# Start of a gated-mix kernel: one piece of K's weights loaded on another queue, the gate vector turned by a padded product, reordered first K pieces with shorter fillers

## Chip, cores and metric

The kernel runs on one core of a Trainium2 chip. The metric is the device time of that core in microseconds (us). Engines: PE is TensorE, PEld its weight loads, DVE is VectorE, ACT is ScalarE, POOL is GpSimd, SP is SyncE; "SPq" and "ACTq" are the queues on which SP and ACT issue DMAs.

## The reference

One input x (2048 x 640, bf16) goes through a linear-attention block A and a mixer with an MLP (block B); a gate mixes the two. Only the first lines of A and the gate matter here:

```python
g = sigmoid((x * gate_w).sum(-1, keepdims=True))
qkv = x @ wqkv                      # 640 -> 3 * 640
q, k, v = ...                       # 32 heads of 20
pq, pk = phi(q), phi(k)             # phi(t) = (t + 1 if t > 0 else exp(t)) + 1e-6
...
return g * a + (1 - g) * b
```

The kernel computes K first: for each of 16 chunks of 128 rows of x, `x_chunk @ wk`, as five products of 128 rows of the contraction (five "pieces" of wk). The gate's logit comes along as a 641st column of wk.

## The kernel before

The start, up to the K products, with cuts marked by `[...]`. Chunk 0 of x is loaded plainly and transposed on PE; chunks 1 to 15 come by seven DMA transposes, all on the SP queue.

```python
load_x(0, 1)                                                  # SP queue
aq.dma_start(g5[:], gate_w.rearrange("(c p) -> c p", p=P))    # aq is the ACT queue
load_wk(sp, 1)
load_wk(aq, 0)
load_wk(aq, 2)
load_wk(sp, 3)
load_wk(aq, 4)
for c0, c1 in ((1, 2), (2, 3), (3, 4), (4, 6), (6, 8), (8, 12), (12, 16)):
    load_xT(c0, c1)                                           # DMA transpose, SP queue
[...]
def k_mm(pt, c, dcs, hfs=(0, 1), last=DC - 1):
    for dc in dcs:
        for hf in hfs:
            n = HD + hf
            nc.tensor.matmul(pt[:, hf, 0:n], lhsT=xT[:, dc, c * P:(c + 1) * P],
                             rhs=wk_sb[:, dc, hf * HD:hf * HD + n], start=(dc == 0), stop=(dc == last))
[...]
def warmup(n, w=TS):        # fillers: products of ones that keep PE busy
    for i in range(n):
        nc.tensor.matmul(warm[:, 1, 0:w], lhsT=one[:, 0:P], rhs=one[:, 0:w], start=True, stop=True)

warmup(6)
warmup(3, P)
kp = pair()
turns = [(pair()[:, 0, :].bitcast(BF16), a, b) for a, b in ((0, 2), (2, DC))]
tg = warm[:, 0, :].bitcast(BF16)
for n, (ptb, a, b) in enumerate(turns):
    for dc in range(a, b):
        nc.tensor.transpose(ptb[:, (dc - a) * P:(dc - a + 1) * P], x_sb[:, 0, dc * P:(dc + 1) * P], ident[:])
    nc.vector.tensor_copy(xT[:, a:b, 0:P], ptb[:, 0:(b - a) * P].rearrange("p (c s) -> p c s", c=b - a))
    if n == 0:
        nc.tensor.transpose(tg[:, 0:DC], g5[:], ident[0:DC, 0:DC])
        nc.vector.tensor_copy(wk_sb[:, :, D], tg[:, 0:DC])
warmup(3, P)
for dc in range(DC):
    k_mm(kp, 0, (dc,))
    if dc < DC - 1:
        warmup(1, 2 * P)
k_evac(kp, 0)
for c in range(1, NCH):
    pt = pair()
    k_mm(pt, c, range(DC))
    k_evac(pt, c)
```

After K come the Q products, then the rest, which the change does not touch.

## Time and profile before

| | before |
|---|---|
| time, median of 3 runs | 265.8 us (265.54 to 266.0) |
| span of the profiled run | 264.0 us |
| first x transpose on PE | 3.66 us |
| first K product / K of chunk 1 / K of chunk 8 | 4.82 / 7.12 / 16.66 us |
| transposed x chunks 8-11 landed | 16.43 us |
| first Q product | 27.56 us |
| full clock granted to PE from | 5.83 us |

Times inside a run count from the start of the span; the landing times are those that the trace records for each DMA. The page of the kernel before begins with the busy time of each engine; its part 4 follows the work that ended last back to its start and gives each engine's share of it:

```profile
span 264.0 us, 4272 instructions
## 1 busy us (share of the span) xinstructions
PE 260.3 (99%) x1744; PEld 161.8 (61%) x1744; DVE 139.5 (53%) x271; ACT 85.1 (32%) x126; POOL 21.9 (8%) x67
...
## 4 chain that ended last, share of the span: by engine, by line
PE 97%; ACT 1%; DVE 0%; issue 0%
```

A chain that is PE to 97% says that what PE starts earlier ends earlier, as long as nothing else comes to be waited for. The timeline of PE in the first 7 us shows what may be saved (start, length, engine, line, operation, tiles, count):

```profile
3.66 0.42 PE L215 MATMUL pp<-ident,x_sb 128*128 128x128 bf16 x2
4.01 0.18 PE L218 MATMUL pp<-ident,g 5*128 5x5 bf16 x1
4.13 0.50 PE L215 MATMUL pp<-ident,x_sb 128*128 128x128 bf16 x3
4.55 0.48 PE L206 MATMUL pp<-const-bfloat16-1.0 128*128 128x128 bf16 x3
4.82 0.74 PE L194 MATMUL pp<-wk_sb,xT 128*128 128x320 bf16 x2
5.36 0.42 PE L206 MATMUL pp<-const-bfloat16-1.0 128*128 128x256 bf16 x1
...
6.74 0.27 PE L206 MATMUL pp<-const-bfloat16-1.0 128*128 128x256 bf16 x1
```

The fillers (L206) stand between the pieces of K (L194). The weight loads of the same stretch show a hole of 0.20 us before the gate vector's, which has 5 rows only:

```profile
3.56 0.25 PEld L215 LDWEIGHTS <-x_sb 128*128 128x128 bf16 x2
4.01 0.10 PEld L218 LDWEIGHTS <-g 5*128 5x128 bf16 x1 [0.20 <-issue]
4.12 0.24 PEld L215 LDWEIGHTS <-x_sb 128*128 128x128 bf16 x3
```

"issue" means that nothing the profile shows was waited for. The timeline of the SP queue shows the first DMA transposes (L121) right behind two pieces of wk (L124):

```profile
0.79 0.39 SPq L118 DMA_DIRECT2D x_sb<-in_A_x_dram  x1
1.25 0.89 SPq L124 DMA_DIRECT2D wk_sb<-in_A_wqkv_dram  x2
2.18 2.73 SPq L121 DMA_TRANSPOSE xT<-in_A_x_dram  x2
```

### The profile page before, as it was taken

To read this page: it belongs to the slowest core of one execution; us is meant where nothing else is said; L and a number is where in the kernel's file an instruction comes from. 1 tells how busy PE (TensorE), PEld (TensorE's weight loads), DVE (VectorE), ACT (ScalarE), POOL (GpSimd) and SP (SyncE) were. 2 spreads that over 40 slices of the span, in tenths; PEclk is the share of its full clock that TensorE was granted. 3 is DMA by queue.
4 is the path that set the end of the run, shared out by engine and by line. 5 is a ranking of instruction groups with operands and counts; after the bars stand their busy time and mean duration, and the time that the engine had idled before them with its cause. 6 is when DMAs were issued, how large, how long until landed. Compare 5 with 4: busy or idle time off the path is not lost.

```text
span 264.0 us, 4272 instructions
## 1 busy us (share of the span) xinstructions
PE 260.3 (99%) x1744; PEld 161.8 (61%) x1744; DVE 139.5 (53%) x271; ACT 85.1 (32%) x126; POOL 21.9 (8%) x67
## 2 busy tenths in 40 slices
PE   8999999999999999999999999999999999999995
PEld 4777555788754654556667555667565576555743
DVE  1688778899948597964503455413356223112132
ACT  1555554321165725612502221412131332142100
POOL 7100120012210040001000001000001000000000
PEclk9999999999999999999999999999999999999999
DMA  7999987016673726700132000051100051100011
GB/s 200 179 208 370 375 252 298 0 29 123 124 101 75 79 51 161 239 0 2 25 75 77 25 0 2 0 99 52 50 0 2 0 101 52 50 0 2 0 50 50
DMA packets 46285, 23.62 MB, mean 89 GB/s; under 512 B 35770, under 2 KB 45626, under 8 KB 46266
## 3 DMA queue, kind: packets, MB, share of 16 engines
q1 hardware_dynamic: 45824, 22.86, 34.1%
q10 hardware_dynamic: 442, 0.49, 0.5%
q8 instruction: 13, 0.21, 0.4%
q14 instruction: 6, 0.05, 0.1%
HBM read 12.21 MB, written 2.62 MB: 56 GB/s over the span
## 4 chain that ended last, share of the span: by engine, by line
PE 97%; ACT 1%; DVE 0%; issue 0%
PE pp L484 21%; PE pp L464 21%; PE pp L194 8%; PE pp L311 8%; PE pp L417 8%; PE pp L448 8%; PE pp L345 8%; PE pp L236 8%; PE pp L206 2%; PE pp L472 1%; PE pp L493 1%; ACT m_sb L385 1%; PE pp L364 1%; PE pp L251 0%; DVE oc L512 0%; PE pp L383 0%
## 5 line engine op out<-in xcount | busy, mean ns | idle before, releaser
L464 PE MATMUL pp<-lnxT,w_sb 128*128 128x512 bf16 x260 | 60.4, 379 | 0.0
L484 PE MATMUL pp<-w_sb,h 128*128 128x256 bf16 (+3 forms) x416 | 58.0, 299 | 0.1
L466 ACT ACTIVATE h<-pp 128x1024 bf16<-128x1024 f32 (+1 forms) x28 | 26.9, 962 | 82.2 <-PE pp L464 82.2
L484 PEld LDWEIGHTS <-h 128*128 128x128 bf16 x416 | 39.3, 98 | 18.0 <-issue 1.3
L464 PEld LDWEIGHTS <-w_sb 128*128 128x128 bf16 x260 | 25.5, 98 | 26.8
L500 DVE SCALAR_TENSOR_TENSOR oc<-pp,omg,x 128x640 bf16<-128x640 f32 x14 | 12.0, 881 | 41.4 <-ACT h2x L475 21.3
L451 DVE SCALAR_TENSOR_TENSOR x<-pp,gate,x 128x640 f32<-128x640 f32 x16 | 13.9, 868 | 29.4 <-PE pp L448 29.4
L420 DVE TENSOR_TENSOR x<-pp,x_sb 128x640 f32<-128x640 f32 x16 | 13.1, 820 | 22.6 <-PE pp L417 22.6
L186 ACT ACTIVATE e<-pp 128x640 bf16<-128x640 f32 (+1 forms) x26 | 21.5, 827 | 9.6 <-PE pp L236 9.6
L448 PE MATMUL pp<-m_sb,pqT 128*128 128x320 bf16 x160 | 24.3, 299 | 0.0
L417 PE MATMUL pp<-w_sb,hsT 128*128 128x320 bf16 x160 | 23.9, 299 | 0.1
L194 PE MATMUL pp<-wk_sb,xT 128*128 128x320 bf16 (+1 forms) x160 | 22.9, 302 | 0.0
L311 PE MATMUL pp<-x_sb,pk 128*128 128x320 bf16 (+1 forms) x160 | 22.3, 300 | 0.0
L236 PE MATMUL pp<-xT,hsT 128*128 128x512 bf16 x100 | 21.7, 379 | 0.0
L311 PEld LDWEIGHTS <-pk 128*128 128x128 bf16 x160 | 18.8, 117 | 3.5
L417 PEld LDWEIGHTS <-hsT 128*128 128x128 bf16 x160 | 15.6, 98 | 8.2 <-issue 0.2
L448 PEld LDWEIGHTS <-pqT 128*128 128x128 bf16 x160 | 15.7, 98 | 7.7
L194 PEld LDWEIGHTS <-xT 128*128 128x128 bf16 x160 | 15.8, 99 | 6.1
L345 PE MATMUL pp<-lnxT,w_sb 128*128 128x512 bf16 x80 | 17.9, 379 | 0.0
L236 PEld LDWEIGHTS <-hsT 128*128 128x128 bf16 x100 | 11.8, 118 | 9.7
L281 POOL TENSOR_SCALAR rstd<-mv 128x4 f32<-128x4 f32 (+1 forms) x11 | 3.4, 314 | 156.5 <-DVE mv L287 156.5
L188 DVE SCALAR_TENSOR_TENSOR pk<-pp,e 128x640 bf16<-128x640 f32 x16 | 13.2, 825 | 1.7
(77 smaller groups left out, 194.9 us busy)
## 6 DMA issues: line engine op xcount, KB each, us to landing
out_dram<-oc SPq DMA_DIRECT2D x14, 160.0 KB, 1.8
w_sb<-in_B_w_dram SPq DMA_DIRECT2D x1, 2080.0 KB, 10.0
w_sb<-in_B_w_dram SPq DMA_DIRECT2D x1, 1296.0 KB, 8.4
x_sb<-in_A_x_dram SPq DMA_DIRECT2D x2, 640.0 KB, 10.4
x_sb<-in_A_x_dram SPq DMA_DIRECT2D x1, 1120.0 KB, 7.9
wo_sb<-in_A_wo_dram SPq DMA_DIRECT2D x6, 160.0 KB, 6.0
w_sb<-in_B_w_dram SPq DMA_DIRECT2D x1, 864.0 KB, 5.7
hsT<-in_A_wqkv_dram SPq DMA_DIRECT2D x1, 800.0 KB, 5.3
```

What stands on the lines that cost most here:

```text
L186: nc.scalar.activation(ev, src, ACT.Exp)
L188: nc.vector.scalar_tensor_tensor(dst, src, 0.0, ev, op0=ALU.max, op1=ALU.add)
L194: nc.tensor.matmul(pt[:, hf, 0:n], lhsT=xT[:, dc, c * P:(c + 1) * P], rhs=wk_sb[:, dc, hf * HD:hf * HD + n], start=(dc == 0), stop=(dc == ...
L236: nc.tensor.matmul(pt[:, t % 2, :], lhsT=wq_sb[:, dc, :].rearrange("p (m j) -> p j m", j=DC)[:, j], rhs=xT[:, dc, t * TS:(t + 1) * TS], st ...
L311: nc.tensor.matmul(pt[:, hf, 0:HD + hf], lhsT=w, rhs=x_sb[:, c, hf * HD:(hf + 1) * HD + hf], start=(c == 0), stop=(c == NCH - 1))
L345: nc.tensor.matmul(pt[:, i, :], lhsT=w, rhs=lnxT[t][:, dc, :], start=(dc == 0), stop=(dc == DC - 1))
L417: nc.tensor.matmul(pt[:, hf, 0:HD], lhsT=hsT[:, fc, 2 + c * P:2 + (c + 1) * P], rhs=w2_sb[:, fc, hf * HD:(hf + 1) * HD], start=(fc == 0), ...
L448: nc.tensor.matmul(pt[:, hf, 0:HD], lhsT=pqT[:, j, c * P:(c + 1) * P], rhs=m_sb[:, j, hf * HD:(hf + 1) * HD], start=(j == 0), stop=(j == D ...
L451: nc.vector.scalar_tensor_tensor(x1, pt[:, :, 0:HD], gate[:, c:c + 1], x1, op0=ALU.mult, op1=ALU.add)
L464: nc.tensor.matmul(pt[:, k, :], lhsT=w3_sb[:, dc, fc * P:(fc + 1) * P], rhs=lnT[:, dc, :], start=(dc == 0), stop=(dc == DC - 1))
L466: nc.scalar.activation(h2[:, 2 * i * TS:(2 * i + n) * TS], pt[:].rearrange("p h e -> p (h e)")[:, 0:n * TS], ACT.Gelu_apprx_tanh)
L484: nc.tensor.matmul(dst, lhsT=st[t]["h2"][:, fc * TS + cc * P:fc * TS + (cc + 1) * P], rhs=w4_sb[:, fc, a:b], start=start and fc == 0, stop ...
```

## The change

The intent is to have PE reach K of chunk 1 earlier: one filler fewer ahead, the gate vector turned without the hole and without a filler waiting for its copy, K's pieces in the order in which they land, shorter fillers between them, and the last piece of wk ahead of the x transposes, so that it lands with the others.

```diff
-    load_wk(aq, 4)
+    load_wk(sp, 4)
[...]
-    def k_mm(pt, c, dcs, hfs=(0, 1), last=DC - 1):
+    def k_mm(pt, c, dcs, first=0, last=DC - 1):
[... start=(dc == first)]
+    k0_order = (1, 0, 3, 2, 4)
[...]
-    warmup(6)
+    nc.vector.memset(g5z[:], 0.0)
+    nc.vector.tensor_copy(g5z[0:DC, :], g5[:])
+    warmup(5)
     warmup(3, P)
     kp = pair()
[... turns keep the whole pair of PSUM banks]
+        if b == DC:
+            nc.tensor.matmul(pt[:, 1, 0:DC], lhsT=g5z[:], rhs=ident[:, 0:DC], start=True, stop=True)
         nc.vector.tensor_copy(xT[:, a:b, 0:P], ptb[:, 0:(b - a) * P].rearrange("p (c s) -> p c s", c=b - a))
-        if n == 0:
-            nc.tensor.transpose(tg[:, 0:DC], g5[:], ident[0:DC, 0:DC])
-            nc.vector.tensor_copy(wk_sb[:, :, D], tg[:, 0:DC])
-    warmup(3, P)
-    for dc in range(DC):
-        k_mm(kp, 0, (dc,))
-        if dc < DC - 1:
-            warmup(1, 2 * P)
+        if b == DC:
+            nc.vector.tensor_copy(wk_sb[:, :, D], pt[:, 1, 0:DC])
+    warmup(4, P)
+    for n, dc in enumerate(k0_order):
+        if n > 1:
+            warmup(1, P)
+        k_mm(kp, 0, (dc,), first=k0_order[0], last=k0_order[-1])
+    warmup(2, P)
```

More of the change, by code (lines that the diff above doesn't have):

```diff
@@ L87 @@
     g5 = const.tile([DC, P], BF16)
+    g5z = const.tile([P, P], BF16)
     mhalf = const.tile([P, CPT], F32)
@@ L188, in phi @@
         nc.vector.scalar_tensor_tensor(dst, src, 0.0, ev, op0=ALU.max, op1=ALU.add)
-    def k_mm(pt, c, dcs, hfs=(0, 1), last=DC - 1):
+    def k_mm(pt, c, dcs, first=0, last=DC - 1):
         for dc in dcs:
-            for hf in hfs:
+            for hf in range(2):
                 n = HD + hf
                 nc.tensor.matmul(pt[:, hf, 0:n], lhsT=xT[:, dc, c * P:(c + 1) * P],
-                                 rhs=wk_sb[:, dc, hf * HD:hf * HD + n], start=(dc == 0), stop=(dc == last))
+                                 rhs=wk_sb[:, dc, hf * HD:hf * HD + n], start=(dc == first), stop=(dc == last))
     def k_evac(pt, c):
@@ L206, in warmup @@
             nc.tensor.matmul(warm[:, 1, 0:w], lhsT=one[:, 0:P], rhs=one[:, 0:w], start=True, stop=True)
-    warmup(6)
+    nc.vector.memset(g5z[:], 0.0)
+    nc.vector.tensor_copy(g5z[0:DC, :], g5[:])
+    warmup(5)
     warmup(3, P)
     kp = pair()
-    turns = [(pair()[:, 0, :].bitcast(BF16), a, b) for a, b in ((0, 2), (2, DC))]
-    tg = warm[:, 0, :].bitcast(BF16)
-    for n, (ptb, a, b) in enumerate(turns):
+    turns = [(pair(), a, b) for a, b in ((0, 2), (2, DC))]
+    for pt, a, b in turns:
+        ptb = pt[:, 0, :].bitcast(BF16)
         for dc in range(a, b):
             nc.tensor.transpose(ptb[:, (dc - a) * P:(dc - a + 1) * P], x_sb[:, 0, dc * P:(dc + 1) * P], ident[:])
+        if b == DC:
+            nc.tensor.matmul(pt[:, 1, 0:DC], lhsT=g5z[:], rhs=ident[:, 0:DC], start=True, stop=True)
         nc.vector.tensor_copy(xT[:, a:b, 0:P], ptb[:, 0:(b - a) * P].rearrange("p (c s) -> p c s", c=b - a))
-        if n == 0:
-            nc.tensor.transpose(tg[:, 0:DC], g5[:], ident[0:DC, 0:DC])
-            nc.vector.tensor_copy(wk_sb[:, :, D], tg[:, 0:DC])
-    warmup(3, P)
-    for dc in range(DC):
-        k_mm(kp, 0, (dc,))
-        if dc < DC - 1:
-            warmup(1, 2 * P)
+        if b == DC:
[6 more added lines that the diff above has]
+    warmup(2, P)
     k_evac(kp, 0)
```

## The prediction

> **What bounds the kernel.** TensorE. The page's chain of work that ended last gives PE 97% of a 264.0 us span; PE is busy 99%. The chain in order of time has PE work without a hole from 7.0 us on. So a gain at the start reaches the end one for one, but only if no later wait eats it. The change touches only the first 7 us (2.7% of the span); a 2% verdict (5.3 us) is out of reach.
>
> **The start now (timeline of PE, DMA landings of the trace).** Warm-up products from 0.83 us; x chunk 0 landed at 3.08; first x transpose 3.66; the 5-row gate turn at 4.01, after a weight-load gap of 0.20 us that the profile calls issue (the gate vector had landed at 2.14, so no data was missing); the next filler began at 4.55, waiting for the DVE copy of the gate column that ended at 4.51. K piece 0 starts at 4.82, piece 4 at 6.85, chunk 1 of K at 7.12. The wk pieces landed: 1 at 4.50, 0 at 4.75, 3 at 5.37, 2 at 5.56, 4 at 6.02. From 4.55 on PE never waits for them: fillers and its own order set the pace. The clock was granted in full only from 5.83.
>
> **Removed.** One cold 512-column filler: 0.43. The row-limited gate turn with its gap and the DVE wait: about 0.14 + 0.13. Fillers in K chunk 0: four of 256 columns become five of 128, about 0.16 net when mostly warm. Added: a DVE memset and copy, hidden, and a 128-row product of 5 columns, under 0.1. Transposes can start at about 3.24. PE then would be ready for K at about 4.27, but piece 1 lands at 4.50, so K starts at about 4.55-4.6. Pieces 1, 0, 3, 2, 4 then run without much waiting; PE is ready for chunk 1 at about 6.75, 0.36 earlier than now.
>
> **What takes it back.** The x transposes are on the SP queue, now behind piece 4 (one SP issue of 0.45 us and 160 KB). The Trainium skill, "DMA: Bandwidth & Descriptors", section "Issuing engines are not separate DMA queues", says the queues share the 16 engines; the trace agrees (DMA 100% busy from 3.5 to 7 us with two queues), so the bytes ahead of the transposes are the same and I estimate a delay of 0 to 0.45 us. Chunk 1 of xT landed at 6.60 (used 7.12). The tightest is chunks 8-11: landed 16.43, used at 16.65, slack 0.22 us only. With PE earlier, chunk 8 becomes DMA-bound: the gain is capped at about 0.17 us minus the delay of the transposes. Net: from 0.2 gained to 0.3 lost.
>
> **Predicted:** 265.6 us, range 265.1 to 266.3; faster by over 2%: 0.01, within 2%: 0.98, slower: 0.01.
>
> **Signs.** Right: transposes near 3.25, no weight-load gap before the gate product, no filler waiting on DVE, K's first piece 4.5-4.6, chunk 1 at 6.75-7.1, and a new PE gap of 0.1-0.6 us before chunk 8 at its landing. Wrong: no gap at chunk 8 and the whole 0.36 us kept; then the transposes' landings moved earlier.
>
> **What could break it.** The Trainium skill, "TensorE: Matmul & The Clock Gate", Part 1, says the clock is released after a busy window of about 3.4 us that runs free of the kernel; here it took 5.0 us from the first product, which agrees. The new idle of 0.25 us before piece 1 might cost a window: K at half speed for another 3.4 us, some 1.5 us lost (a 5% risk). A shift of the window from run to run also moves either kernel by some tenths. Late landing of x shifts everything.

## The result

The changed kernel took 265.88 us in the median of 4 runs, the kernel before 265.70 us in 4 runs. One of the four changed runs, the profiled one, took 704.76 us: PE ran at a little over a third of its pace from beginning to end (most K products start 0.405 us after the one before, where the other runs have 0.136) and the trace holds no clock record at all. It is a slow run and is left out of the times; its three fast companions took 265.69 to 265.98 us (median 265.79). The ratio of the fast runs is 1.0003, 95% interval 0.9984 to 1.0023. A ratio is formed from the mean times of fast runs, so it is not quite the ratio of the medians.

Run again in a later set, beside the kernel before (run e1 below), the change gave 266.35 us against 265.85, ratio 1.0022 (1.0009 to 1.0035). The second is a loss of 0.2% clear of noise. Its profile is used from here on.

```profile
span 264.5 us, 4260 instructions
...
## 4 chain that ended last, share of the span: by engine, by line
PE 91%; SPq 3%; DMA 3%; ACT 1%; issue 1%; DVE 0%
```

The chain is no longer PE alone: 6% of it is now the SP queue and a DMA. (The trace lacks 17 of the 1745 matmul records, so its PE count is not a finding.) The start of PE did what was intended:

```profile
3.23 0.74 PE L219 MATMUL pp<-ident,x_sb 128*128 128x128 bf16 x5
3.77 0.21 PE L221 MATMUL pp<-ident,g5z 128*128 128x5 bf16 x1
3.84 0.59 PE L208 MATMUL pp<-const-bfloat16-1.0 128*128 128x128 bf16 x4
4.21 1.29 PE L195 MATMUL pp<-wk_sb,xT 128*128 128x320 bf16 x4
...
6.88 0.57 PE L195 MATMUL pp<-wk_sb,xT 128*128 128x320 bf16 x3
```

The five transposes follow each other, the padded gate product comes 0.11 us after the last of them starts, the fillers wait for nothing, and K starts 0.61 us earlier (4.21 against 4.82). By chunk 1 the lead is 0.24 us (6.88 against 7.12), since the clock became full later in this run (6.27 us against 5.83): until then K's products stand about 0.27 us apart, afterwards 0.14. No wait for a piece shows in this trace. Ten microseconds on, the timeline shows this:

```profile
15.32 1.25 PE L195 MATMUL pp<-wk_sb,xT 128*128 128x320 bf16 x8
17.18 1.54 PE L195 MATMUL pp<-wk_sb,xT 128*128 128x320 bf16 x10 [0.60 <-DMA xT<-in_A_x_dram]
```

In the same stretch before, PE runs through:

```profile
15.29 3.43 PE L194 MATMUL pp<-wk_sb,xT 128*128 128x320 bf16 x24
```

The product at 17.18 is the first of chunk 8. It starts 0.90 us after the one before it, where 0.136 is the normal distance: 0.76 us lost. The lead of 0.24 has become a lag of 0.52 (17.18 against 16.66); the first Q product lags by 0.53 (28.09 against 27.56), and the span by 0.51. So the account closes: the start gains 0.24, the wait before chunk 8 takes 0.76, and nothing else moves.

The chain in order of time says where that wait comes from (start, length, what):

```profile
...
1.71 0.42 SPq L125
2.14 0.04 issue
2.18 0.43 SPq L125
2.61 0.04 issue
2.66 1.29 SPq L122
...
9.71 7.42 DMA xT<-in_A_x_dram
17.13 0.05 issue
17.18 11.07 PE pp L195 x80
```

It is one row of issues on the SP queue: x, three pieces of wk (L125, the last two are shown), then the transposes (L122, the first is shown), and at last the flight of the transpose of chunks 8-11. The last L125, 0.43 us, is the one that the change put there. The issue of 8-11 began at 9.71 instead of 9.41, 0.30 later, and its flight took 7.42 us instead of 7.03, 0.39 longer; it landed at 17.13 instead of 16.43. In both traces that flight is the longest among the x transposes whose landing is told (view of the tile xT, before and then e1):

```profile
DMA to landing us min/median/max: 3.7/4.6/7.0
```

```profile
DMA to landing us min/median/max: 3.4/4.5/7.4
```

### The profile page after: what moved, and what is told of

Read it like the earlier page. It is cut to its first block, busy times and chain, and to the rows that moved or that the text cites. A ratio compares the mean times of both kernels' runs of the same rounds, so it can differ in the third digit from the quotient of the medians.

```text
span 703.0 us, 4277 instructions
## 1 busy us (share of the span) xinstructions
PE 699.5 (99%) x1745; PEld 281.3 (40%) x1745; DVE 141.4 (20%) x273; ACT 85.7 (12%) x126; POOL 21.6 (3%) x67
## 4 chain that ended last, share of the span: by engine, by line
PE 99%; DVE 0%; issue 0%
PE pp L470 22%; PE pp L490 22%; PE pp L195 9%; PE pp L351 9%; PE pp L317 8%; PE pp L242 8%; PE pp L454 8%; PE pp L423 8%; PE pp L389 1%; PE pp L478 1%; PE pp L499 1%; PE pp L208 1%; PE pp L370 1%; PE pp L257 0%; PE pp L219 0%; PE pp L269 0%
## 5 line engine op out<-in xcount | busy, mean ns | idle before, releaser
L470 PE MATMUL pp<-lnxT,w_sb 128*128 128x512 bf16 x260 | 161.2, 837 | 0.0
L490 PE MATMUL pp<-w_sb,h 128*128 128x256 bf16 (+3 forms) x416 | 155.9, 609 | 0.0
L490 PEld LDWEIGHTS <-h 128*128 128x128 bf16 x416 | 70.7, 173 | 84.4 <-issue 62.7
L470 PEld LDWEIGHTS <-w_sb 128*128 128x128 bf16 x260 | 45.9, 176 | 98.1 <-issue 98.1
L454 PE MATMUL pp<-m_sb,pqT 128*128 128x320 bf16 x160 | 63.4, 610 | 0.0
L423 PE MATMUL pp<-w_sb,hsT 128*128 128x320 bf16 x160 | 62.4, 605 | 0.0
L195 PE MATMUL pp<-wk_sb,xT 128*128 128x320 bf16 (+1 forms) x160 | 60.7, 616 | 0.0
L317 PE MATMUL pp<-x_sb,pk 128*128 128x320 bf16 (+1 forms) x160 | 59.9, 614 | 0.0
L242 PE MATMUL pp<-xT,hsT 128*128 128x512 bf16 x100 | 59.8, 835 | 0.0
L351 PE MATMUL pp<-lnxT,w_sb 128*128 128x512 bf16 x80 | 48.5, 838 | 0.0
L423 PEld LDWEIGHTS <-hsT 128*128 128x128 bf16 x160 | 27.2, 170 | 37.2 <-issue 37.0
L426 DVE TENSOR_TENSOR x<-pp,x_sb 128x640 f32<-128x640 f32 x16 | 13.2, 825 | 109.1 <-PE pp L423 109.1
L242 PEld LDWEIGHTS <-hsT 128*128 128x128 bf16 x100 | 18.7, 187 | 40.4 <-issue 40.4
L351 PEld LDWEIGHTS <-w_sb 128*128 128x128 bf16 x80 | 13.9, 174 | 32.9 <-issue 32.5
```

What stands on the lines that cost most here:

```text
L242: nc.tensor.matmul(pt[:, t % 2, :], lhsT=wq_sb[:, dc, :].rearrange("p (m j) -> p j m", j=DC)[:, j], rhs=xT[:, dc, t * TS:(t + 1) * TS], st ...
L317: nc.tensor.matmul(pt[:, hf, 0:HD + hf], lhsT=w, rhs=x_sb[:, c, hf * HD:(hf + 1) * HD + hf], start=(c == 0), stop=(c == NCH - 1))
L351: nc.tensor.matmul(pt[:, i, :], lhsT=w, rhs=lnxT[t][:, dc, :], start=(dc == 0), stop=(dc == DC - 1))
L423: nc.tensor.matmul(pt[:, hf, 0:HD], lhsT=hsT[:, fc, 2 + c * P:2 + (c + 1) * P], rhs=w2_sb[:, fc, hf * HD:(hf + 1) * HD], start=(fc == 0), ...
L426: nc.vector.tensor_tensor(x1[:].rearrange("p (h e) -> p h e", h=2), pt[:, :, 0:HD], x_sb[:, c, 0:D].rearrange("p (h e) -> p h e", h=2), op ...
L454: nc.tensor.matmul(pt[:, hf, 0:HD], lhsT=pqT[:, j, c * P:(c + 1) * P], rhs=m_sb[:, j, hf * HD:(hf + 1) * HD], start=(j == 0), stop=(j == D ...
```

## The experiments

Three theories stood against each other at first. A: the start gains, and the wait for the transposed x takes it back. B: the start gains nothing, because waits for the pieces took the fillers' place. C: the clock becomes full later. All twelve runs gave correct results. Each profile is one execution, and not always a typical one: it was the fastest of its run's six in e2 and e12 and the slowest in e3, e5 and e6. e1 to e4, e5 to e8 and e9 to e12 ran on one chip each, with the kernel before alongside (medians 265.85, 265.83 and 265.79 us).

| run | full clock | chunk 1 | 8-11 landed | chunk 8 | first Q | median | ratio to before |
|---|---|---|---|---|---|---|---|
| before | 5.83 | 7.12 | 16.43 | 16.66 | 27.56 | | |
| e1 change again | 6.27 | 6.88 | 17.13 | 17.18 | 28.09 | 266.35 | 1.0022 |
| e2 piece 4 on ACT | 4.24 | 6.52 | 16.47 | 16.51 | 27.42 | 266.01 | 1.0005 |
| e3 queue move alone | 5.59 | 7.57 | 17.70 | 17.75 | 28.66 | 266.40 | 1.0018 |
| e4 change, 8-11 split | 5.84 | 6.83 | 15.16 (8-9) | 16.60 | 27.50 | 265.77 | 0.9998 |
| e5 change, short warm-ups | 4.67 | 6.97 | 17.07 | 17.12 | 28.03 | 267.38 | 1.0061 |
| e6 e5 with piece 4 on ACT | 3.97 | 7.09 | 16.95 | 17.00 | 27.91 | 266.96 | 1.0041 |
| e7 before, short warm-ups | 3.84 | 6.66 | 17.40 | 17.45 | 28.36 | 266.92 | 1.0039 |
| e8 five-row gate | 3.44 | 6.66 | 17.22 | 17.27 | 28.18 | 266.35 | one look |
| e9 change, 4-7 merged | 4.56 | 7.72 | 16.43 | 18.48 | 29.38 | 267.59 | 1.0072 |
| e10 e2, 8-11 split | 5.24 | 6.95 | 14.06 (8-9) | 16.50 | 27.39 | 265.69 | 0.9992 |
| e11 e2, 4-7 merged | 6.34 | 6.93 | 15.70 | 17.86 | 28.76 | 267.23 | 1.0050 |
| e12 before, 8-11 split | 3.93 | 6.68 | 14.57 (8-9) | 16.34 | 27.24 | 265.95 | 0.9998 |

In every run in which chunk 8 waits (e1, e2, e3, e5 to e8), it starts 0.04 to 0.05 us after 8-11 landed, whatever chunk 1 did: chunk 1 lies anywhere from 6.52 to 7.57. And the first Q product moves by the later landing minus 0.17 us, the cap that the prediction had worked out. For e1, e2, e3, e5, e6, e7 and e8 that gives +0.53, -0.13, +1.10, +0.47, +0.35, +0.80 and +0.62; measured were +0.53, -0.14, +1.10, +0.47, +0.35, +0.80 and +0.62. This is arithmetic once chunk 8 waits; what the agreement shows is that nothing between chunk 8 and Q waits again.

### e1: the change again

No edit.

> The changed kernel once more, for a profile in the fast state. Theory A (eaten by the x transposes): the first K product starts at 4.5-4.6 us (before 4.82), chunk 1 of K at 6.75-7.1 (before 7.12), but PE stands idle before chunk 8 until its transposed x lands, and chunk 8 starts at 16.5-16.9 (before 16.65), the Q products at 27.6-28.0 (before 27.72). Rival B (nothing gained at the start, waits for the wk pieces took the fillers' place): chunk 1 at 7.0 or later and no idle time before chunk 8. Rival C (clock): the granted clock becomes full later than 5.83 us, so K chunk 0 runs at half pace for longer. All: time within 0.2% of before.

Theory A's picture came, at its far end: the first K product earlier still than expected (4.21, because piece 1 landed at 4.01, not 4.50), chunk 1 at 6.88, chunk 8 at 17.18, above the 16.9 that I had allowed. Rival B falls for the start, since chunk 1 did come earlier. Rival C has a share: the full clock came at 6.27, 0.44 later than in the trace of before, and the start gained all the same. The time, 0.22% over before, was just beyond the 0.2% that all theories expected.

### e2: the change without the queue move

```diff
-    load_wk(sp, 4)
+    load_wk(aq, 4)
```

> The change without its queue move (piece 4 stays on the ACT queue). Theory A: the transposes land as before (chunk 1 of xT 6.6, chunks 8-11 16.4), chunk 1 of K at about 6.7-6.8, chunk 8 held to about 16.5 by its landing: Q products at 27.5-27.6, up to 0.2 us better than before. Rival B: piece 4 lands last at 6.0 and holds K chunk 0, chunk 1 no earlier than 7.0. Rival C: as the clock falls.

With piece 4 back on ACT, 8-11 landed at 16.47, as before. Chunk 1 came at 6.52, 0.60 earlier than before; PE then stood before chunk 8 all the same (start-to-start 0.58, so 0.44 lost) and kept 0.14 us at the first Q product. The timeline line:

```profile
16.51 2.22 PE L195 MATMUL pp<-wk_sb,xT 128*128 128x320 bf16 x15 [0.28 <-DMA xT<-in_A_x_dram]
```

So even a larger gain at the start is capped by this landing. In the times it is not seen: 1.0005 (0.9992 to 1.0018).

### e3: the queue move alone

```diff
-    load_wk(aq, 4)
+    load_wk(sp, 4)
```

in the kernel before.

> The kernel before with the queue move alone. Theory A: PE's first 7 us as before (chunk 1 of K at 7.1), piece 4 lands no later than 6.0, chunks 8-11 of xT land 0 to 0.5 us later than 16.43; if over 0.2 us later, PE waits for them, and the Q products start at 27.7-28.0. Rival B: no wait before chunk 8, Q products at 27.72 as before.

The move alone costs: ratio 1.0018 (1.0005 to 1.0031), close to the whole change's 1.0022. Its profile is worse than expected: pieces 3, 2 and 4 landed only at 6.26, 6.50 and 6.78 (expected: no later than 6.0), PE waited for them as well, and 8-11 landed at 17.70. The late pieces are not a mark of the move: in e1 and e8, with the same move, piece 4 landed at 5.78 and 6.02, in e9 at 6.99, and in e6 without the move at 6.52.

### e4: the change with the transpose of 8-11 split

```diff
-(6, 8), (8, 12), (12, 16)
+(6, 8), (8, 10), (10, 12), (12, 16)
```

> The change with the transpose of x chunks 8-11 split in two, so that 8-9 land first. Theory A: 8-9 land at about 14.5-15.2, PE does not wait before chunk 8, and the whole gain at the start is kept: chunk 8 at 16.2-16.4, Q products at 27.3-27.5, about 0.3 us better than before. Rival B: nothing changes against the changed kernel.

The wait before chunk 8 is gone. PE runs through it, as in the kernel before:

```profile
15.23 3.43 PE L195 MATMUL pp<-wk_sb,xT 128*128 128x320 bf16 x24
```

The time falls from 266.35 (e1, same chip) to 265.77 us, with no overlap between the runs of the two (266.19 to 266.85, 265.72 to 265.95). This takes away what made PE wait, and nothing else of PE's work: the wait was the cost. It is not the expected gain on the kernel before (0.9998), since the wait moved forward to chunk 4, which now starts at the landing of 4-5 at 11.09. The chain in order of time is the same row on the SP queue, cut off at an earlier transpose:

```profile
...
2.66 1.29 SPq L122
...
6.63 4.46 DMA xT<-in_A_x_dram
11.09 0.04 issue
11.13 16.52 PE pp L195 x120
```

### e12: control, the kernel before with the same split

The edit of e4, in the kernel before.

> Control: the kernel before with x chunks 8-11 split the same way. Theory A: PE did not wait before chunk 8 there, so nothing is gained: Q products at 27.5-27.7, time within 0.1% of before. If it gains as much as the two runs with the changed start, the split alone is the cause and the start is worth nothing.

The split gives the kernel before nothing: 0.9998 (0.9984 to 1.0012), 265.95 against 265.79 us. It helps the changed kernel only, as A says. Its one profile shows a better first Q product (27.24) than expected; there the clock was full at 3.93 instead of 5.83, which brings chunk 1 from 7.12 to 6.68 without any change of code in the start.

### e10: both hindrances taken away

The edits of e2 and e4 together.

> Piece 4 back on the ACT queue and x chunks 8-11 transposed as 8-9 and 10-11: both the later start of the transposes and the wait before chunk 8 are taken away. Theory A: chunk 1 of K at 6.5-6.8, no gap over 0.2 before chunk 4 or 8, Q products at 27.1-27.4 (before 27.56), time 0.2 to 0.4 us better than before. Rival B: time as before or worse.

The best median of all, 265.69 us against 265.79, but not clear of noise: 0.9992 (0.9978 to 1.0005). The expected 0.2 to 0.4 us did not come. In its profile piece 4 landed at 6.36 and chunk 1 of x at 6.90, so chunk 1 started at 6.95, only 0.17 us better than before. Here rival B is right in part: shorter fillers bring PE to the edge of what has landed.

### e9 and e11: 4-7 transposed at once

```diff
-(4, 6), (6, 8), (8, 12)
+(4, 8), (8, 12)
```

in the change (e9) and in e2 (e11).

> The changed kernel with the transposes of x chunks 4-5 and 6-7 merged into one of four chunks, one fewer in the row. Theory A: 8-11 land 1 us or more before 17.1, the gap before chunk 8 is under 0.2 us; 4-7 land at 10.9-11.4, which may leave a gap of up to 0.5 before chunk 4; Q products at 27.2-27.7, better than the changed kernel's 28.09. Rival B (the wait before chunk 8 is not what costs): Q at 28 as before.

> Piece 4 on the ACT queue and 4-7 transposed at once. Theory A: 4-7 land at 10.5-11.0, a gap of 0-0.4 before chunk 4, none before chunk 8, Q products at 27.1-27.5, time 0.1 to 0.4 us better than before. Rival B: time as before or worse.

I had misjudged the merged transpose: it landed at 12.97 (e9) and 12.35 (e11), not at about 11, and PE waited before chunk 4 (start-to-start 1.33 and 1.52 us). The waits view of e11, with total, times and longest, all from this one place:

```profile
PEld L195 <- DMA xT<-in_A_x_dram: 1.5, 1, 1.5
PE pp L195 <- DMA xT<-in_A_x_dram: 1.2, 1, 1.2
```

As improvements both fail; as tests they add a dose. A transpose that lands later makes the kernel slower by about that much (1.0050 and 1.0072); in the profiled run of e9 PE had also waited 1.3 us for late pieces, but that adds nothing by itself: chunk 4 starts at the landing of 4-7 in any case.

### e8: the gate vector on 5 rows again

```diff
-nc.tensor.matmul(pt[:, 1, 0:DC], lhsT=g5z[:], rhs=ident[:, 0:DC], start=True, stop=True)
+nc.tensor.matmul(pt[:, 1, 0:DC], lhsT=g5[:], rhs=ident[0:DC, 0:DC], start=True, stop=True)
```

> The changed kernel with the gate vector's product on 5 rows again instead of the zero-padded 128, all else as changed: the weight-load gap before it returns (0.1-0.2 us on the weight-load row), K's first product 0.1-0.3 us later than 4.21; the transposes, the gap before chunk 8 and the time hardly move, because chunk 8 waits for its landing at about 17.1. Rival: no gap, then the row count was not the reason for it in the kernel before.

The weight loads of e1, then those of e8:

```profile
3.23 0.47 PEld L219 LDWEIGHTS <-x_sb 128*128 128x128 bf16 x5
3.66 0.15 PEld L221 LDWEIGHTS <-g5z 128*128 128x128 bf16 x1
```

```profile
3.17 0.44 PEld L219 LDWEIGHTS <-x_sb 128*128 128x128 bf16 x5
3.71 0.09 PEld L221 LDWEIGHTS <-g 5*128 5x128 bf16 x1
```

With 128 rows the load starts while the one before it still runs; with 5 rows it starts 0.10 us after that one ended. So the hole comes back with the 5-row load, and the padded product does what it was meant to do. (The edit also changes the tile that is read, g5 instead of g5z. No data was missing in either: the copy of g5 into g5z was done by 2.4 us in e1 and 2.9 us in e8.) The Trainium skill, "TensorE: Matmul & The Clock Gate", section "Step-by-step: what each phase is for", says that PE pulls a weight load ahead of running matmuls if the row groups do not conflict or if it goes to the background buffer; a 5-row load that waits fits that, though which of the two conditions fails here no run shows. K's first product came at 4.30, within what was expected, but it waited there for piece 1 (landed 4.26), so that part tells nothing. The time, 266.35 us in one run of unknown state on another chip, equals e1's median, as it should when chunk 8 waits for its landing (17.22) all the same.

### e5, e6, e7: the instruction fetch (theory D)

Every trace but that of the slow run has 16 KB packets of instruction fetch, the first between 13.2 and 16.4 us, and after it transposed packets of 256 bytes that took 0.5 to 1.6 us instead of some 20 ns. Theory D is that the fetch holds up the transposes of 8-11; rival E, that the long packets are the transposes' own. The Trainium skill, "Runtime: NRT & Kernel Launch", section "Instruction fetch mechanics", says that engines refill their instructions in blocks of 16 KiB, 256 instructions, by DMA; the thirteen fetches of e1 lie 252 PE instructions apart in the mean, the last six 248 to 259 (earlier ones 211 to 287), which agrees. I tried to move the first one by more, but shorter, warm-up products:

```diff
-    warmup(5)
+    warmup(20, P)
```

in the change (e5), in e2 (e6), and from `warmup(6)` to `warmup(24, P)` in the kernel before (e7).

> The changed kernel with its five 512-column warm-up products written as twenty of 128 columns: the same columns of work, 30 more PE instructions (with the weight loads). Theory D (the 16 KB packet of PE's instruction fetch, at 14.9 us in the changed kernel, holds up the transposes of x chunks 8-11; in each trace so far transposed packets of 256 bytes that took 0.5 to 1.2 us follow it): the fetch comes 1 to 3 us earlier, 8-11 land about 1 us earlier (15.5-16.2 instead of 17.1), the PE gap before chunk 8 falls from 0.9 to under 0.3 us, Q products at 27.2-27.6 instead of 28.09, time about 0.5 us better than the changed kernel. Rival E (the stragglers are of the transposes themselves, the fetch only happens to be there): 8-11 still land at about 17.1 and the gap stays at 0.7-0.9.

> The same fetch shift and piece 4 back on the ACT queue. Theories A and D: 8-11 land at 15.0-15.7, no PE gap before chunk 8, the whole gain of the start is kept: Q products at 27.0-27.2, 0.3 to 0.5 us better than before, the best of all so far. Rival E: a gap of 0.5-0.6 before chunk 8 as in the run with piece 4 on ACT alone, Q at 27.4.

> The kernel before with its six 512-column warm-up products written as 24 of 128 columns (36 more PE instructions). Theory D: 8-11 of xT land at about 15-15.7 instead of 16.43, but PE never waited for them there, so the time stays within 0.1% of before. Rival E: they land at 16.4; time the same.

The expected gain did not come in any of the three. In e5 the first fetch did not move (14.81 against 14.89) and 8-11 landed at 17.07: the test failed, and rival E's numbers came. In e6 and e7 it moved from 14.21 (e2) and 14.18 (before) to 13.56 and 13.25, and 8-11 landed later (16.95 and 17.40), not earlier. In e7 the DMA view of the 2.2 us from 13.2 us on, in 40 slices, shows the transfer at rest after the fetch (the instruction queue's packet is in the last line):

```profile
GB/s 586 279 270 275 177 0 0 0 0 0 0 0 0 0 0 0 0 5 9 5 9 9 9 9 9 9 9 9 9 9 9 14 177 284 284 298 289 293 293 293
...
q8 instruction: 1, 0.02, 2.7%
```

But transposed packets also stood still where no fetch was near (e8 at 7.2 us, up to 1.15 us; e3, e6 and e9 between 5 and 6 us). The trace of the slow run goes further. PE was so slow there that the first fetch came only at 27.27 us; yet 37 transposed packets took 0.5 to 0.97 us before it, and 8-11, issued at 9.90, landed at 17.11, as in e1 (17.13). It is one trace, of a slow run, but its SP issues and landings are like those of the fast runs. So a landing this late needs neither a fetch nor PE at its full pace; that the fetch adds to it in other runs is not shown.

All three were slower than expected by far, and half of that or more came later in the kernel (of the lag of the span, 2.48, 1.44 and 1.64 us, only 0.47, 0.35 and 0.80 were there at the first Q product). In e5 the fetch of 77.5 us (e1) came at 71.8 us. The DMA views of 70.5 to 76.5 us of e1 and then of e5, with the median time to landing of the transposes of `gs` in the last line:

```profile
GB/s 179 220 217 210 197 53 0 0 24 227 297 288 232 25 0 0 0 53 266 294 285 186 9 0 0 55 0 0 0 5 179 292 288 268 60 0 0 0 0 142
...
wk_sb<-gs SPq DMA_TRANSPOSE x3, 2.4
```

```profile
GB/s 213 220 215 215 147 16 0 0 203 263 273 218 14 0 0 0 0 0 0 9 9 9 10 10 174 65 96 213 266 230 55 5 17 29 173 9 0 0 0 0
...
q8 instruction: 1, 0.02, 1.7%
...
wk_sb<-gs SPq DMA_TRANSPOSE x2, 4.5
```

In e1 the fetch falls on a transpose that nobody waits for yet; in e5 it falls on those of `gs`, which the products at L370 need at once:

```profile
79.17 1.59 PE L370 MATMUL pp<-wk_sb,m_sb 128*128 128x120 bf16 x30 [1.87 <-DVE ln L307]
```

In e1 the same products start at 77.19 without a wait. (The profile names DVE as the releaser; the last transpose of `gs` landed at 78.97, which fits better.) The products there start 2.25, 1.32 and 1.06 us after the one before in e5, e6 and e7, and 0.22 us in all the other profiles except the slow run's. The code at that place is the same, so here the fetch's place in time is the likely cause in three of three; it is not shown, since no run moved the fetch alone.

## Why the prediction was right or wrong

- **The size, "265.6 us, range 265.1 to 266.3": right in the first set, just missed in the second.** 265.88 us lies in it, and "within 2%" held. The centre was on the wrong side, though: a small gain was put in the middle, and the repeated run, 266.35 us, lies just above the range. That the first number fell inside may be in part luck: the delay of 8-11 was 0.64 to 0.79 us, above the predicted 0.45, in every trace that has the changed start, the queue move and the transposes as in the change (e1, e5, e8 and the slow run). The fast runs of the first set left no trace.
- **"PE ready for chunk 1 at about 6.75, 0.36 earlier": nearly right.** 6.88, 0.24 earlier; with piece 4 on ACT 6.52 in one trace, where the clock was full at 4.24. K started at 4.21 instead of 4.5-4.6: I took the landing of piece 1 (4.50) as fixed, and over the thirteen traces other than the slow one it was 3.96 to 4.55.
- **"Chunk 8 becomes DMA-bound: the gain is capped at about 0.17 us minus the delay of the transposes": right, and shown.** Seven runs obey it within 0.01 us, the split (e4) takes the wait away and gives back 0.58 us of the median, and the same split gives the kernel before nothing (e12).
- **"A delay of 0 to 0.45 us": the term that was mis-sized.** It measured 0.70 us in e1: 0.30 from the later issue and 0.39 from the longer flight. 0.17 - 0.70 = -0.53 is what e1 lost. The issue part lies within the estimate, whose top was one issue, and it is a mark of the queue move: the transpose of 8-11 (of 8-9 where split) was issued at 9.71 to 10.02 us in the six traces with the move and at 9.38 to 9.55 in the six without, the merged ones left out. The flight overshot: 7.03 us before and 7.09 in e2, but 7.2 to 8.0 us in the seven other traces with 8-11 whole and 4-7 not merged, e6 and e7 without the move among them. I argued from the bytes, which are the same on either queue, as the Trainium skill, "DMA: Bandwidth & Descriptors", section "Issuing engines are not separate DMA queues", would have it; that page also names the issue time as what a second queue saves, and the issue time, 0.43 us on a row with no slack, is the part of the delay that the move explains. What made the flight longer stays open.
- **The signs: all but two as stated.** Transposes at 3.23, no hole before the gate product, no filler waiting for DVE, chunk 1 at 6.88, a gap before chunk 8. But K's first product came at 4.21 instead of 4.5-4.6, and the gap took 0.76 us instead of 0.1 to 0.6.
- **The clock: a fair warning, no loss in the end.** The full clock came between 3.44 and 6.34 us over the thirteen traces other than the slow one. The same start code had chunk 1 at 7.12 and at 6.68 (before and e12) with the clock at 5.83 and 3.93, a difference larger than what the change gained there in e1. In e1 the later full clock took part of the lead, 0.61 us at K's start and 0.24 at chunk 1; the wait before chunk 8 would have eaten it anyway.

Open: why the first fast runs of the change (265.69 to 265.98) did better than e1 (266.19 to 266.85); what stops transposed packets, with or without a fetch near; what the 704.76 us run was.

## What to carry to other kernels

Before making a start faster, look for the next landing that it will run into: the slack of each later load (here 0.22 us for chunks 8-11, of which 0.17 could be used) is the most that the start can gain. On a queue that feeds a chain of transfers without slack, an inserted issue delays the rest even when the bytes are the same in all: here 0.43 us of issue made 8-11 start 0.30 us later in e1. Put it on the queue that has time. And adding instructions moved later instruction fetches (from 77.5 to 71.8 us in e5): when a harmless change at the start makes a far-off stage slower, look at which transfer a fetch now falls on, as a suspect to be tested.

## What the Trainium skill lacked or had wrong

- "Runtime: NRT & Kernel Launch", "Instruction fetch mechanics", calls a fetch across a block boundary mostly hidden. Here, in the three kernels whose fourth fetch came at about 71.7 us instead of 76.6 to 78.8, PE started the products after it 1.1 to 2.3 us after the one before instead of 0.22; the fetch is the likely cause, not shown.
- No page speaks of packets of a DMA transpose that stand still. Here packets of 256 bytes took 0.5 to 1.6 us instead of some 20 ns: in each of the thirteen traces other than the slow one at least twelve in the 2 us after the first 16 KB fetch, but up to 35 before it (e3), and 37 in the slow run, far from any fetch.
- "TensorE: Matmul & The Clock Gate", Part 1, puts the first 3.4 us of work at the half clock, and explains the spread, half a microsecond either way, by a window that runs free of the kernel. Here the spread was larger: the full clock came 2.6 us after the first product in e8 (3.44 against 0.83 us), sooner than 3.4 us, and 5.5 us after it in e11.
- The same page warns of a clock that stays low for some tens of us; the run of 704.76 us had most K products 0.405 us after the one before instead of 0.136, all other stages slowed likewise, and no clock record. No page has that.
- "DMA: Bandwidth & Descriptors" gives for issuing a DMA transpose only cycle counts, in a table on a later chip, the one from HBM for small tiles: here it took 1.3 to 1.4 us of the SP queue for one chunk of 128 x 640, 3.2 to 4.9 us for four. One of four chunks took longer to land than I had expected: 4-7 at once landed at 12.4 to 13.0 us, where 4-5 and 6-7 had landed at 10.4 and 12.5 us before.
